# Another written-out order for the first part of an attention and Fourier-mixing kernel

## The chip, the cores and the metric

The kernel runs on one core of a Trainium2 chip. The metric is the time of one execution in device microseconds (us). The core has five engines that run side by side and wait for one another by semaphores: PE (matrix products), ACT (elementwise functions), DVE (elementwise and reductions), POOL (elementwise), and SP, which here only issues transfers (DMA). Products land in eight banks of an accumulation memory, and another engine has to carry them off before a bank is used again.

## The reference

An attention block with random features, then a bridge, a Fourier mix, a normalisation and a two-layer MLP, all in float32:

```python
q_s, k_s = q * scale, k * scale                  # (8, 8, 576, 64), omega (128, 64)
def phi(x):
    h = einsum('bhsd,md->bhsm', x, omega) - sum(x * x, -1, keepdims=True) / 2
    return exp(h - max(h, -1, keepdims=True)) / sqrt(128)
kv, z = einsum('bhsm,bhsd->bhmd', phi(k_s), v), sum(phi(k_s), 2)
out = einsum('bhsm,bhmd->bhsd', phi(q_s), kv) / (einsum('bhsm,bhm->bhs', phi(q_s), z) + 1e-6)

x = heads of out side by side                     # (8, 576, 512)
u = x + real(fft(fft(x, axis=1), axis=2))
un = (u - mean(u)) / sqrt(var(u) + 1e-6)          # over the last axis
result = u + maximum(un @ w_ch1, 0) @ w_ch2       # (512, 2048), (2048, 512)
```

The two weight matrices arrive as float64.

## The kernel before, in words

The kernel has two parts, one after the other, each with an order of its own.

**The first part** ends at about 418 us. For each of the 8 batches it takes the 8 heads in 4 pairs (`attn`). A pair's k and q are loaded by SP (L499, L502) into `kq` and turned on PE (L642); the turned tiles are evicted as `kqT` (L658 on ACT, L656 on DVE). L737 forms the products with omega, L679 (DVE) the maxima, L696 (ACT) the exponentials `e`; L772 sums `kv`, L820 and L828 form the output, and L845 (ACT) or L849 (DVE) divide it into `x`, a tile that holds all heads of a batch (`x0` and `x1` in turn). The chip's omega itself is loaded by L518 and turned once at L620 (`first`). `warm` (L611) is six products of a tile of zeros, whose results nobody reads; each shows as two passes in the trace.

When the four pairs of a batch are done, `mix` does its Fourier transform by table products. It folds rows that mirror each other (L876 to L905 on DVE or POOL), multiplies by cosine and sine tables along the model axis (L939, result `y`, evicted at L969) and along the sequence (L999 and L1010). `residual` combines the two products of each of three chunks: L1048 (ACT) copies one out of its bank, L1053 and L1056 (DVE) form sum and difference, L1065 and L1066 (DVE or POOL) add them to `x`. What is then in `x` goes to a buffer `us` in device memory by SP (L1080). A middle slice goes by L1035 into a buffer `uh`, and L1091 copies that, in mirrored order, from `uh` into `us`: it has to wait for both stores of L1035 to land.

Beside that the first part narrows the weights from float64 to float32 (`narrow`: L564 on POOL or L566 on ACT, then L569 to L578 on DVE, then L582), forms sums of blocks of the second weight matrix (`w2_parts`, L1550), and passes four blocks of 128 tokens through the MLP in the plain way (`plain_of`: L1233 turns, L1299 is the first layer, L1281 or L1283 the relu, L1324 the second layer, L1338 adds the residual, L1115 stores the result). The last of these blocks is what PE does last in the first part. For the next 4 times 512 tokens it also normalises twelve half-blocks ahead (`ahead`, L1662 to L1676): ACT sums (L1662, L1665), POOL works out the factor (L1667 to L1669), ACT scales (L1671), DVE turns (L1674), SP stores (L1676). These use free `kq`, `kqT` and `ur2` tiles.

**The order of the first part** is written out by hand, as text. The work is a set of generators (streams); each gives one step at a time, with the engines on which the step may run. `Listing.run` holds a list of streams, each with its next step, and `PICKS` says which to take next: one character for each step, whose position in an alphabet is 36 times the choice of engine plus the stream's place in the list. `BANKS` is the bank of each step that takes one. `FORMS` says, for PE steps that can be cut in several ways, which cut: W is whole, C cuts the output into two halves of 64 columns, R and Q are the two cuts of L737 (20 passes over 128 columns or 32 over 64 for a group of four), and lower case letters stand for the middle of a mix. `BETWEEN` places the pieces of `ahead` after so many steps taken. Every engine executes its instructions in that order, so an instruction that waits holds what is behind it on its engine:

```python
def picked(text, n):
    if n == 1:
        return [divmod(DIGITS.index(c), 36) for c in text]
...
    listing.run(
        [first(), loads(), loads_v(), load_tables(), frames(), plain_norms(), mixing()]
        + [pairs(i) for i in range(NS)]
        + [w2_parts(), weight_sums(), block_norms(0, mlpp), plain(), weights(), warm()],
        picked(PICKS, 1),
        BANKS,
        betweens(BETWEEN),
    )
    early.close()
```

**The second part** takes the remaining tokens through the MLP by products of block sums in which seven products stand for eight (L1794 and L1946 first layer, L2247 second layer). `early.close()` gives up the tiles of the first part's loads, attention, mix and plain MLP, and the second part's tiles (`hid`, `so5`, `so6`, `so3`, `rx`, `s`, `wl`) lie in the same memory. Its first instructions are L2367 (`wash`, which clears banks), L1794, L1826 and L1819 (ACT, evictions, the second into `s`), L1749 (DVE and POOL, sums of weight blocks into `rx` and `so`), L1837 (DVE), L1924 (ACT) and L1946. Its loads of second-layer weights are L2142. It has order texts of its own (`PICKS2`, `BANKS2`, `BETWEEN2`).

Of the kernel before, what the change touches and what calls it, by code (L numbers as in the profile page):

```python
# [41 lines left out]
class Clock(NamedTuple):  # L42
# [23 lines left out]


PICKS = (
    "40e0fff03eafdaege3OcdceefdcOdeccfgda37ghj0gjj7hlP79aj7ik97i8S7efhjffeHldffiehdjfdOihgihidaKedbhhciff"
    "ecgOfeejdfdPdeeedgifdffdefd8aiii88jhd8jP8b99i8e8jcddghjgheiifcOcdciieicgPgdefJcdghbkededfgcRbggb79ij"  # L70
    "8hi7hjafN9Haj9gfffeg8eif8hcej1jccc7ehidbhffLigebfbe6766gggfcbjahj9Ofghhjj8dQkkgT6jghff8de6dUjfhbgegh"
    "cefhafjUf8jgciSjOckkhjakkaeikggjlioklnhSgodoXON7l7l6nnj9icadc97cibf98ejH88a7edhMlhkmjjaQVijihkkfplSm"
    "okliljjilVaghVhnmljkmpjkhhnmkimlgglmbjpjjQ9d9alafhhdjlaMdjback0j766k7lh4g896ck6gkki77gij5ijhgj6dimni"
    "3ndjgi6Kc4jldlKikbkaijLhf75dcjlmklk36ci45jciekajkkkk5kihokeaeoLaioNlencidonbSiljjcmjjkboijTUUhgcfkik"
    "hiflkmeFF99nol5m8jT7naabda89Rbj97ecdl8cjilOgifkQb4acahg57ebbgabgdjkdTkk6eceebb5f9dg4R6ce486ggg6egfhh"
    "fg4g9egf5cbdhgPRhhcgjhggejigibLmHnbedijj6NOb7biihi9bgihMkaffPa8cijdhbdghbaeibNefffacjicigifi99975ih5"
    "jgj8699ajfg6g7fgefd65bO6Kalkkgd5jgjikagfldliPJpeoaeeefgdejadgilgScljiii5e65k56kl57k7j67S9lilk9gliih6"
    "ffkgec4fg4dbgg7fedaiP5gfbheefilddddddeghg9kbfncgghcfkkafkagGngb65p5Hopoj4bhoanbelli68bjjl5b7dlhighhi"
    "lflhpkgiWomjknmmmkimnjbjhn9jkmFKkfFgedccff6Wf7idUVhi8Th3fogbqp8fgmkeSdjna7ckenoghmnmffnjeo79q6547oa4"
    "nlkpd7aceonnc8blSVicilbhmjim8fh7SnnIl5mUkfjgfhhfhihg8ghfbS4kjf83j4lllb79jei8mnkblfnmmiolpilOUi9Mh5l5"  # L80
    "pmnaem79jjVmkbblek5iji9a9kffTgjikhiShfgjafhgfigh4g50PPP0ba5Pdh9dghdK77hgfdcbg8OO988jMehefibjjkellfcc"
    "PcdhQMihfQcffbKCf82b3c98cbcdcd6a299efgddbJaGQQbefLa9ecf74gg986HRgf9idg8kQeheff7be6ff2e5cc8fbcgdKP8f8"
    "9hN9Lc999bddcHcNb7Oc9effegd7ibhQeQ8haf7ccghhlUikhHW5lWmm5dkMQGM71fS6d1gdb99747ifddhIfdhhdhfdbihgiljn"
    "gWgijgg93ekKl8kEhIIbT3jjKgkb9k9eTfhkhlje34m49974iG66h68faHe6e7a79982975aI94a39c8cM8b4aa7ab984fge8eLM"
    "98b86ce8PbFPc9cbe6cKPf3a9b94fIdIQeJKbd876eJPdc5fNb7ffbf9JSS8RiLa4a7gPbajfgg8gdfhg2i2787Hf6OcdIN5d3LH"
    "accd46ddeKK72dJc7bbaa4bb9a9bc7c0777dghhdf7Bfddebd76ff1fddIe9949438686bc6aca85348dHcG7a5be957b55d1544"
    "9Gc1F5a9a68446344584584E59189970955888574443113301110"
)

BANKS = (  # L90
    "0102346120164024306243643016204164024320632462014021604606245062345042604670426420340267407231640260"
    "4524016460620240674206206415704602546064320143607264506402346234062732017426042106147026740260462462"
    "0410652604632452017205467402624060404256174302642060245016745202642016420634520520650162505605260250"
    "1675602501605204672016204567627450264102316742067460260462045642062637230724672402630145420640106240"
    "5264023026731602454230412046450416725730620424670121726154305610207453"
)

FORMS = (  # L100
# [6 lines left out]
)  # L107


# [2354 lines left out]
```

## Time and profile before

| | us |
|---|---|
| median of 3 runs | 1117.52 |
| lowest and highest run | 1115.76, 1120.93 |
| the profiled execution, its own time | 1114.35 |
| its span, from the first to the last instruction | 1112.6 |
| first part (end of the last L1324) | 418.5 |
| PE busy | 1093.4 |
| DVE busy | 885.9 |
| ACT busy | 539.1 |
| POOL busy | 390.4 |

The durations of the profile come from the one profiled execution. In its rows, times are microseconds from the start of the span unless they are marked as ns; a row of the timeline gives start, duration, engine, line and operation, output and inputs by their names in the program, the tile sizes, how many instructions run in a row are grouped (x12), and, in brackets, how long the engine stood idle before and what released it. PEld is the loading of stationary tiles into PE, beside the products; SPq and ACTq mark the issue of a transfer. The granted clock is the share of full speed at which PE was allowed to run; it is 1.00 throughout. T in the text is the end of the last L1324, where the first part's work on PE ends.

### The profile page before, as it was taken

What the parts mean: (1) busy time and instruction counts of PE and PEld (TensorE: products, weight loads), DVE (VectorE), ACT (ScalarE), POOL (GpSimd) and SP (SyncE); (2) the same over time, 40 slices, a digit from 0 to 9 for tenths busy, and PEclk for the clock granted to TensorE, in tenths of its full rate; (3) what the DMA queues carried; (4) which work ended last, traced back from release to release, by engine and by line L of the source; (5) the groups of instructions that cost most, each with busy time, mean ns of one, the idle gap of its engine ahead of it and who ended that gap; (6) DMA issues with size and microseconds to landing.
All of it is one profiled execution on the core that took longest, in us unless ns stands there. A gap on an engine that the chain in (4) does not pass through costs nothing.

```text
span 1112.6 us, 41751 instructions
## 1 busy us (share of the span) xinstructions
PE 1093.4 (98%) x17507; PEld 934.7 (84%) x17507; DVE 885.9 (80%) x1685; ACT 539.1 (48%) x1644; POOL 390.4 (35%) x404
## 2 busy tenths in 40 slices
PE   8999999999999999999999999999999999999998
PEld 6788888878869666799998888998667999667998
DVE  6999999996676766688697777898667898668895
ACT  6998898856635464624214453223563223341221
POOL 2343443644473346634513455000365000152000
PEclk9999999999999999999999999999999999999999
DMA  7856767575675668798898768757678757556553
GB/s 230 229 183 182 241 182 220 162 212 160 221 231 187 188 169 314 236 300 287 247 303 300 211 200 260 213 155 237 206 216 262 220 154 223 167 158 220 151 158 113
DMA packets 196588, 236.77 MB, mean 213 GB/s; under 512 B 53808, under 2 KB 120624, under 8 KB 196400
## 3 DMA queue, kind: packets, MB, share of 16 engines
q1 hardware_dynamic: 195904, 233.83, 68.7%
q8 instruction: 138, 2.26, 0.9%
q14 instruction: 50, 0.41, 0.1%
q10 hardware_dynamic: 496, 0.26, 0.1%
HBM read 182.13 MB, written 56.10 MB: 214 GB/s over the span
## 4 chain that ended last, share of the span: by engine, by line
PE 90%; ACT 4%; DVE 3%; DMA 2%; issue 1%; SPq 0%; POOL 0%; DVEq 0%; ACTq 0%
PE banks L2247 30%; PE banks L1794 27%; PE banks L642 5%; PE banks L737 5%; PE banks L1324 5%; PE banks L1299 4%; PE banks L1946 4%; PE banks L772 3%; PE banks L820 2%; ACT e L696 2%; PE banks L999 1%; PE banks L939 1%; DMA kq<-in_q_dram 1%; DVE nmx L679 1%; PE banks L953 1%
## 5 line engine op out<-in xcount | busy, mean ns | idle before, releaser
L2247 PE MATMUL banks<-wl,sums 128*64 128x128 f32 x3584 | 217.5, 273 | 0.1
L2247 PEld LDWEIGHTS banks<-wl,sums 128*64 128x64 f32 x3584 | 201.6, 137 | 2.1 <-issue 0.5
L696 ACT ACTIVATE e<-banks,nmx 128x128 f32<-128x128 f32 x576 | 164.3, 426 | 21.8 <-DVE nmx L679 20.8
L679 DVE TENSOR_REDUCE nmx<-banks 128x8 f32<-128x1024 f32 (+1 forms) x96 | 89.3, 951 | 18.5 <-PE banks L737 15.4
L2247 PE MATMUL banks<-wl,hid 128*64 128x128 f32 x1536 | 99.0, 273 | 0.5 <-DVE part L2222 0.5
L2247 PEld LDWEIGHTS banks<-wl,hid 128*64 128x64 f32 x1536 | 88.0, 137 | 1.8 <-DVE part L2222 0.7
L1794 PE MATMUL banks<-unw,wxw 128*64 128x256 f32 x704 | 86.2, 379 | 0.0
L2217 ACT ACTIVATE s<-banks 128x128 f32<-128x128 f32 x112 | 30.9, 277 | 109.8 <-PE banks L2247 109.8
L737 PE MATMUL banks<-om,kqT 64*64 64x128 f32 (+1 forms) x1804 | 80.1, 276 | 2.5 <-issue 1.1
L737 PEld LDWEIGHTS banks<-om,kqT 64*64 64x64 f32 (+1 forms) x1804 | 66.2, 148 | 13.0 <-issue 4.8
L2247 PE MATMUL banks<-wl,hx 128*64 128x128 f32 x1152 | 73.6, 273 | 0.4 <-DVE part L2222 0.4
L1794 PEld LDWEIGHTS banks<-unw,wxw 128*64 128x64 f32 x704 | 53.3, 137 | 22.0
L1794 PE MATMUL banks<-rx,wxw 128*64 128x256 f32 x576 | 71.7, 379 | 0.0
L1794 PE MATMUL banks<-ttw,wxw 128*64 128x256 f32 x576 | 70.6, 379 | 0.0
L1819 ACT ACTIVATE s<-banks 128x512 f32<-128x512 f32 x65 | 38.5, 596 | 64.9 <-PE banks L1794 59.8
L2247 PEld LDWEIGHTS banks<-wl,hx 128*64 128x64 f32 x1152 | 65.4, 137 | 1.2 <-DVE part L2222 0.6
L1299 PE MATMUL banks<-unT,w 128*64 128x128 f32 (+1 forms) x720 | 64.7, 276 | 1.8 <-DVE qeT L656 1.8
L582 POOL TENSOR_TENSOR w<-w,raw 128x512 f32<-128x512 f32 x28 | 37.7, 1357 | 77.4 <-DVE raw L576 74.5
L2296 POOL TENSOR_TENSOR more<-more,part 128x512 f32<-128x512 f32 x2 | 2.7, 1336 | 172.8 <-ACT part L2289 172.8
L1299 PEld LDWEIGHTS banks<-unT,w 128*64 128x64 f32 (+1 forms) x720 | 58.6, 160 | 5.3 <-issue 2.3
L1794 PEld LDWEIGHTS banks<-rx,wxw 128*64 128x64 f32 x576 | 44.0, 137 | 17.6
L1794 PEld LDWEIGHTS banks<-ttw,wxw 128*64 128x64 f32 x576 | 44.0, 137 | 17.6
(289 smaller groups left out, 2413.3 us busy)
## 6 DMA issues: line engine op xcount, KB each, us to landing
wl<-w2l SPq DMA_DIRECT2D x245, 256.0 KB, 3.9
wxw<-w1x SPq DMA_DIRECT2D x120, 256.0 KB, 3.2
raw<-in_moe_w_ch_dram SPq DMA_DIRECT2D x32, 512.0 KB, 5.3
kq<-in_k_dram SPq DMA_DIRECT2D x32, 288.0 KB, 4.4
kq<-in_q_dram SPq DMA_DIRECT2D x32, 288.0 KB, 4.7
vd<-in_v_dram SPq DMA_DIRECT2D x32, 288.0 KB, 5.5
ur<-us SPq DMA_DIRECT2D x30, 256.0 KB, 4.6
w2l<-sums SPq DMA_DIRECT2D x14, 512.0 KB, 4.9
```

Of the source, the lines that this page charges most:

```text
L582: eng.tensor_tensor(out=dst, in0=dst, in1=lof, op=ALU.add)
L642: nc.tensor.transpose(ps[:, (j - j0) * 128 : (j - j0 + 1) * 128], src(j), ident[:])
L679: nc.vector.tensor_reduce(nmx[:, :, 0:num], pps[:, :, 0 : MF * num].rearrange("p b (c m) -> p b c m", m=MF), axis=AX.X, op=ALU.max, negate ...
L696: nc.scalar.activation(out=e[:, c + (i if num == 1 else 0), :], in_=pps[:, i, MF * c : MF * c + MF], func=AF.Exp, bias=nmx[:, i, c : c + 1],)
L737: nc.tensor.matmul(pps[cols, c, MF * m : MF * m + MF], lhsT=kqT[rows, j, cols], rhs=om2[rows, :],)
L772: nc.tensor.matmul(kvp[cols, i, 0 : D + 1], lhsT=feature(r)[rows, cols], rhs=vds[n % NV][rows, r, :], start=(r == 0), stop=(r == R - 1),)
L1299: nc.tensor.matmul(hp[cols, 0:TP], lhsT=w1[:, dc, 128 * fc : 128 * fc + 128][:, cols], rhs=unTs[key][:, dc, :], start=(dc == 0), stop=(dc ...
L1324: nc.tensor.matmul(yp[cols, 0:DM], lhsT=hs[fc][:, 128 * i : 128 * i + 128][:, cols], rhs=w2[:, fc, :], start=(fc == 0), stop=(fc == NFC - ...
L1794: nc.tensor.matmul(ps[half, span * f : span * f + span].rearrange("f (b q) -> f b q", q=Q), lhsT=left[:, P * f : P * f + P][:, half], rhs= ...
L1819: nc.scalar.activation(out=s[:], in_=ps, func=AF.Copy)
L1946: nc.tensor.matmul(cell[half].rearrange("f t (b q) -> f t b q", q=Q), lhsT=w[:, d, col : col + 128][:, half], rhs=right[:, :, d].rearrange ...
L2247: nc.tensor.matmul(ps[half, 0:128], lhsT=left[:, f][:, half], rhs=wls[head(j), i, n][:, f], start=start and f == 0, stop=(f == 3), skip_gr ...
```

## The change

The change replaces the three texts `PICKS`, `BANKS` and `FORMS` of the first part. It changes no function, and `BETWEEN` and the texts of the second part stay. Cut to the first and last lines of each text, the diff is:

```diff
 PICKS = (
-    "40e0fff03eafdaege3OcdceefdcOdeccfgda37ghj0gjj7hlP79aj7ik97i8S7efhjffeHldffiehdjfdOihgihidaKedbhhciff"
...
-    "98b86ce8PbFPc9cbe6cKPf3a9b94fIdIQeJKbd876eJPdc5fNb7ffbf9JSS8RiLa4a7gPbajfgg8gdfhg2i2787Hf6OcdIN5d3LH"
-    "accd46ddeKK72dJc7bbaa4bb9a9bc7c0777dghhdf7Bfddebd76ff1fddIe9949438686bc6aca85348dHcG7a5be957b55d1544"
-    "9Gc1F5a9a68446344584584E59189970955888574443113301110"
+    "0ff0e5cedce04aadbcN9dcffaddhfS9ibbbKdd4Pg9hagdfgKb9ggahbd9gMadgccfbiiiaifjS9fdeic8gada1ebggb9gi7RJb7"
...
+    "a57cKC7McF57ab7aa6ccRee7edhLahagghffdcKg1Qbd9d2hehhfee21bKcPgQQ8PPP9Oeadde1259E47eDNeeOeeeeeOeOeObac"
+    "ceNadeed3cddNcdMM4123a8G646826J9abcdefg506GeddhQagPAf67cheij7jHdj79T3aMj86gb9egacQabI59ccc478a3b57c2"
+    "a895423345888557206477H8H737715355F652556562314232010"
 )
 BANKS = (
-    "0102346120164024306243643016204164024320632462014021604606245062345042604670426420340267407231640260"
...
+    "3041346021064104260174062306201464602367026426450642014202640141050640264236204206126042301672042064"
...
 )
 FORMS = (
-    "5W 2R W Q 2W 2Q 2W Q W Q 2W Q W C Q 3W 2R 3W 3Q W C 2W Q 3W C 2Q 2W Q W Q 3W 4Q C 2W Q 5W 3Q C W WR 3W WQ W R "
...
-    "2R 2Q 9W 5W czC 6C 2W WQ 5C CQ W C Ccz 3C W 3C Ccz 2C Ccz 9W 3W"
+    "5W 2R W R 2W 2Q 2W 2Q 4W Q C Q 3W 2R 3W 3Q C 4W Q 2W C 2Q 2W 2R 4W 4Q C 3W Q 4W 3R C W WR 3W WQ W Q 2Ccz Q W 2R "
...
+    "C 2Ccz 9W W 3C Ccz 9W 3Q 7W WQ 5C CQ 4Q Ccz 6W 2Q 3C Ccz 2C 2R 2Q C 9W 8W czC 9C 9C 4C 4W CQ 5W WQ C 2Ccz czC 3C"
 )
```

Since the orders are data, what the change does is read from the instructions of the two built programs, engine by engine:

- On PE, the transposition of omega (L620) stands ahead of the six products of `warm` instead of behind them and four transposes of k.
- L1299 runs in 128 whole and 256 half-width instructions instead of 152 and 208, L1324 in 42 whole and 44 half instead of 56 and 16, L737 in 224 wide and 704 narrow groups' passes instead of 250 and 652.
- Work that may run on several engines is shared out anew: L564 (POOL) 28 instead of 8 and L566 (ACT) 4 instead of 24; L876 on POOL 11 instead of 5 and on DVE 5 instead of 11; L845 (ACT) 80 instead of 40; L1283 (ACT) 32 instead of 44.
- Near the end of the first part fewer L1324 stand behind the last mix: 12 instead of 32. On ACT the last two pieces of `ahead` stand ahead of the L1048 of the mix's last two chunks, and on SP the last stores are, in order: two L1035, L1091, two L1676, L1115, and four L1080.

The line numbers of this text are those of the program before; in the changed one they are one lower from the texts on, because `PICKS` is a line shorter.

More of the change, by code (lines that the diff above doesn't have):

```diff
@@ L68 @@
 PICKS = (
-    "40e0fff03eafdaege3OcdceefdcOdeccfgda37ghj0gjj7hlP79aj7ik97i8S7efhjffeHldffiehdjfdOihgihidaKedbhhciff"
[L70 to L83, printed above, removed]
@@ L84 @@
-    "gWgijgg93ekKl8kEhIIbT3jjKgkb9k9eTfhkhlje34m49974iG66h68faHe6e7a79982975aI94a39c8cM8b4aa7ab984fge8eLM"
-    "98b86ce8PbFPc9cbe6cKPf3a9b94fIdIQeJKbd876eJPdc5fNb7ffbf9JSS8RiLa4a7gPbajfgg8gdfhg2i2787Hf6OcdIN5d3LH"
-    "accd46ddeKK72dJc7bbaa4bb9a9bc7c0777dghhdf7Bfddebd76ff1fddIe9949438686bc6aca85348dHcG7a5be957b55d1544"
-    "9Gc1F5a9a68446344584584E59189970955888574443113301110"
+    "0ff0e5cedce04aadbcN9dcffaddhfS9ibbbKdd4Pg9hagdfgKb9ggahbd9gMadgccfbiiiaifjS9fdeic8gada1ebggb9gi7RJb7"
+    "79h8fbj0k9fj9bh7Ih9iaacahbcfbc8ahiekalf6hgc6hghi89kJkhcfjjTbdiihgjgJceiRdidlkgdeeigim8UcldcddgjcddeR"
@@ new lines @@
+    "8hcebO99ahgig9h9ibigggf98h1hdaR9g6eidhiiiije8i6h7diSdjdjdeaHQi9bhg9dh7kg9mmcjab6afminUi9l9kfjgf8icJf"
+    "f7giibUfmXjcOhmedj69lggji6jkghj7ebmc9n6gekjelcmnnklkcbjaf7jmRIlkbgibidRcfifljHQelilmeVTjdeTaikhldklm"
+    "lhkVaelfgeljliafdfgfQfSkhHea7hhaldjemdkkkTh9lfNQdTggfjjj9abk89gjl505j6d8kddkc87j5djlc7cakba56kicajcd"
+    "mcmddnccJRmRd5Idf3SgIbk9K6fllmangmfnk6aQd8hkjleggmmleenkm6k8HnbfTlk8emallmWjdjkjlggmmfhnjm3SjgeRi9dj"
+    "ldkkchhffjchljLTgVkljfgclkJkTkj96ccm86l5Heod8ak3Hjakjkjkjk89ki9hbg6effffa5fcf4Qfgc6Kbgdhabci8cahLdgf"
@@ new lines @@
+    "de6O84fNf56fgiO96hh8k6Sffhg9i9bJkadhbdjighT6aSejii6a8hdcfj7egfdcdbOb8edf8cdecbgjcjhdbgmmicaGh7Qn4eGI"
+    "7L7khjNci7fbghhRih79cd7mhnaibkonoagU6ihdgJfGIQjaddi55ialcmWbgiimUegjlc8iVdWmWffbkdjdeei9ckaG7d68al99"
+    "kilO7gij4bMd7dcf7eci5idhcc4jdibedejlhfl6df6lebNjfkNjgdjd9kgUf5gehilklba9499fmdfllVhill8akmlbnib6nkih"
+    "lll8fHihk7ejjaclUkhdglikjhll84higl5felh6iWgNiNi3njYbgcdcPnbdicpqigqnWP9apedcknkpfilSaiekgnhbnXHdimim"
+    "fi4lJcmllkT6f8Ucllcf9cfhmVhbfomo9paeeRmjmdVfnng65gk45jieli3jUbfk5k7Ql7hmm77gOidjlilnjkV55oNghnfflmnj"
@@ new lines @@
+    "lmc7cOgfj55ikk8fkmmjeJbgQglcmmeSkghhkkjglhmbi9ecmeli9g4iijdcicciiihghffi5miQjae7Pkck9EfRafejkSggejQM"
+    "eeaOa8fLb7ee49d9dacdef8cf7agafgP5Qg8edf8K8efe9hdJObcdhRQdg9dbd9fgfdKcP9bgcdgcabP9PPaaP49aeLccddecc1c"
+    "879ef7bbeecbb3ebdfdM6L8ef0ef16LhK1gThe6k66k2M66dHdgiFM8bhhe4jdjflc6aglm99dfM6lWPbe2Sc5D84kajNaiijfQb"
+    "8a5kjhlgllJddge4mUlcfM8OMfSe9hc4ea9f7f8g82919a56P27cFa792ccI9d685897aebJcc5Ib8b8fgegd98a28efNd6dMfOa"
+    "a57cKC7McF57ab7aa6ccRee7edhLahagghffdcKg1Qbd9d2hehhfee21bKcPgQQ8PPP9Oeadde1259E47eDNeeOeeeeeOeOeObac"
@@ L94 @@
-    "1675602501605204672016204567627450264102316742067460260462045642062637230724672402630145420640106240"
-    "5264023026731602454230412046450416725730620424670121726154305610207453"
+    "3041346021064104260174062306201464602367026426450642014202640141050640264236204206126042301672042064"
+    "2014016260462042672042620451356250642314036702674260140642306034021673045624610421640726346204604202"
+    "6067167240632405134750643260204624604625736503642060264701450724604672726014012562040126073640620603"
@@ L96 @@
+    "7242060231206421065206450142065026406351074626410167406202456240642643725732013640746527464214506254"
+    "3046206457234065234236024623627045010760462257236410571734054134616406"
 )
 FORMS = (
[6 rows of a table removed]
[5 rows of a table added]
 )
```

2 lines of the change are left out of this document (removed), and 7 rows, old and new, of the table FORMS.

## The prediction

> **What bounds the kernel now.** I read the head of the page first, then a table of busy time by stretch, then the timeline at the two ends of the first part. The page's first two parts and the engine line of its chain:
>
> ```profile
> span 1112.6 us, 41751 instructions
> PE 1093.4 (98%) x17507; PEld 934.7 (84%) x17507; DVE 885.9 (80%) x1685; ACT 539.1 (48%) x1644; POOL 390.4 (35%) x404
> PE 90%; ACT 4%; DVE 3%; DMA 2%; issue 1%; SPq 0%; POOL 0%; DVEq 0%; ACTq 0%
> ```
>
> The next view is split at 100 and 420 us; the first part ends a little before 420. Its columns are stretch, length, then busy time of PE, PEld, DVE, ACT and POOL, the granted clock, DMA share and GB/s.
>
> ```profile
> 0.00:100.00 100.00, 90.96 (x2042) 76.47 (x2046) 85.47 (x172) 86.16 (x314) 35.66 (x44) 1.00 0.72 207
> 100.00:420.00 320.00, 315.19 (x5595) 259.82 (x5587) 260.16 (x595) 213.93 (x739) 150.91 (x166) 1.00 0.64 197
> ```
>
> The reader is to see that PE sets the time, that PE idles only 100 - 90.96 = 9.0 us in the first stretch and 320 - 315.19 = 4.8 us in the second, and that PE's instructions in the part that changes aren't shortened by a slow clock. A new order of the same steps has these to win: 13.8 us of PE idle, and whatever PE work the new forms save. It can lose at any place where PE is now covered. So I looked for places where it uncovers PE: the start, and the seam to the second part.
>
> **Forms and turns.** In the built programs the number of places in the first part where PE changes its tile shape goes from 206 to 182. What one change costs, and what a form costs:
>
> ```profile
> 74.49 0.60 PE L642 MATMUL banks<-ident,e 128*128 128x128 f32 x4
> 74.92 0.27 PE L642 MATMUL banks<-ident,kq 128*128 128x128 f32 x1
> 75.03 0.60 PE L642 MATMUL banks<-ident,e 128*128 128x128 f32 x4
> 75.56 0.85 PE L820 MATMUL banks<-kv,qeT 128*64 128x65 f32 x21
> 398.37 1.95 PE L1299 MATMUL banks<-unT,w 128*64 128x128 f32 x32
> 402.85 1.95 PE L1299 MATMUL banks<-unT,w 128*128 128x128 f32 x16
> ```
>
> Four transposes followed by the same shape start 74.92 - 74.49 = 0.43 us apart from what follows; four followed by a 64-column tile, 75.56 - 75.03 = 0.53. A turn costs 0.10 us; 24 fewer give **-2.4 us**. The same L1299 step takes 1.95 us as 16 whole or 32 half instructions, so I cost the form itself at nothing. Its ends are -1, since some turns lie beside a wait, and -3.4, as turns between other shapes may cost more.
>
> **The start.** The rows of the timeline from 0 to 8 us, and, for the tile `om`, the time from issue to landing:
>
> ```profile
> 0.72 0.47 ACTq L518 DMA_DIRECT2D om<-in_omega_dram  x1
> 1.04 2.93 PE L611 MATMUL banks<-ur 128*128 128x128 f32 x12 [1.04 <-DVE ur L520]
> 3.90 0.64 PE L642 MATMUL banks<-ident,kq 128*128 128x128 f32 x4
> 4.37 0.27 PE L620 MATMUL banks<-ident,om 128*128 128x128 f32 x1
> 5.13 0.77 PE L642 MATMUL banks<-ident,kq 128*128 128x128 f32 x5 [0.48 <-DMA kq<-in_q_dram]
> DMA to landing us min/median/max: 3.2/3.2/3.2
> ```
>
> Before, PE fills the wait for the first loads with the six products of L611 (12 passes), and these end as k lands. In the changed program L620, which needs omega, stands first on PE, and the twelve passes stand behind it. Omega lands at 0.72 + 3.2 = 3.9, L620 takes 0.27, the passes again up to 2.93 - 0.27 = 2.7, so the first transposes of k start near 6.9 instead of 3.90: 3.0 later. The 0.48 us wait for q goes, as q has landed by then: **+2.5 us**. If the passes ran at the pace of 0.11 us that the transposes above show ((0.60 - 0.27) / 3) they would take 1.3, and the loss would be 1.1; 3.0 is the other end. L611's pace, 0.24 at its start, argues for the high side.
>
> **Inside the first part.** The change moves elementwise work between engines. The counts are of the built programs: L564 on POOL 8 to 28, L566 on ACT 24 to 4 (the same narrowing step), L876 on POOL 5 to 11 and on DVE 11 to 5; the other moves nearly cancel on POOL. One instruction of each costs:
>
> ```profile
> L564 POOL TENSOR_SCALAR w<-raw 128x512 f32<-128x512 f32 x8 | 12.9, 1613 | 19.8 <-DMA raw<-in_moe_w_ch_dram 19.8
> L876 POOL TENSOR_TENSOR half<-x 128x1024 f32<-128x1024 f32 x5 | 11.8, 2360 | 8.7 <-DVE mid L915 5.1 <-DMA kq<-in_q_dram 2.0 <-DVE rden L837 0.7
> L566 ACT ACTIVATE w<-raw 128x512 f32<-128x512 f32 x24 | 18.4, 777 | 3.9 <-DMA raw<-in_moe_w_ch_dram 3.9
> L876 DVE TENSOR_TENSOR half<-x 128x1024 f32<-128x1024 f32 x11 | 14.7, 1340 | 0.2
> L574 DVE TENSOR_SCALAR sign<-w x32: 426/428/1430, 15.7 to 242.6; 128x512 uint32<-128x512 uint32 x32
> ```
>
> POOL gains 20 x 1.61 + 6 x 2.36 = 46 us, against its 187 (35.66 + 150.91) in 420; it stays under 60%, so its own time is free while nobody waits for it. ACT sheds 20 x 0.78 = 16 us (much of it taken back by evictions, which are written out by hand as well), DVE 6 x 1.34 = 8. ACT is at 86% and DVE at 85% in the first 100 us, where PE's idle is largest, so this should shorten PE's waits for them: I take **-5 us**, about a third of the 13.8. No row prices it: -12 (nearly all idle goes) and +5 are its ends. For the upper end: L574 took 428 ns in the median and 1430 at worst, so something holds DVE now and then, and with a quarter more of POOL's work that may grow, on every such line. The Trainium skill's "SBUF — State Buffer", under "SBUF: two separate sides", says that DVE with two operands from that memory (or in a fast mode) and GpSimd lock one pair of ports for a whole instruction, the loser blocked; taken for each of the 26 added POOL instructions, with one of their lengths each, that speaks against this change by 46 us of DVE time. This trace shows one-instruction delays on L574 of up to 1.0 us, and a median without any.
>
> **The seam.** The second part's text is unchanged, but its tiles lie in memory that the first part held. In both built programs these instructions wait for every transfer that reads a first-part tile: ACT's first L1819, DVE's and POOL's first L1749, SP's first L2142. How that looks before:
>
> ```profile
> 404.64 13.90 PE L1324 MATMUL banks<-w,ht 128*128 128x512 f32 x32
> 416.58 0.53 SPq L1676 DMA_DIRECT2D turned<-kqT  x1
> 418.57 0.69 DVE L1338 TENSOR_TENSOR ur<-ur,banks 128x512 f32<-128x512 f32 x1 [2.02 <-PE banks L1324]
> 419.25 0.69 DVE L1749 TENSOR_TENSOR rx<-w 128x512 f32<-128x512 f32 x1
> 420.92 0.60 ACT L1819 ACTIVATE s<-banks 128x512 f32<-128x512 f32 x1 [0.29 <-PE banks L1794]
> 422.92 1.04 PE L1794 MATMUL banks<-unT,w1s 128*64 128x128 f32 x16
> 424.43 0.69 DVE L1837 TENSOR_TENSOR hid<-banks,s 128x512 f32<-128x512 f32 x1 [1.48 <-PE banks L1794]
> 426.40 1.90 PE L1946 MATMUL banks<-unT,w 128*64 128x256 f32 x16
> ```
>
> Call T the end of the last L1324: 404.64 + 13.90 = 418.5. The last transfer of the first part is L1676 (issued 416.58, landed 2.4 us later by the row of its kind below): T + 0.5. So the gate is open when PE gets there, thanks to 13.9 us of L1324 behind the last mix. In the changed order only twelve L1324 (12 x 13.90 / 32 = 5.2 us) stand behind the mix's last product, and everything that the mix leaves to do comes after. Its prices:
>
> ```profile
> 412.04 0.61 ACT L1662 ACTIVATE kqT<-kqT 128x512 bf16<-128x512 f32 x1
> 415.84 0.71 DVE L1674 STREAM_TRANSPOSE kqT<-kqT 128x512 f32<-128x512 f32 x1 [1.16 <-ACT kqT L1671]
> 402.15 0.52 DVE L1053 SCALAR_TENSOR_TENSOR bmp<-banks,bmp 128x65 f32<-128x65 f32 x2
> 402.54 0.28 DVE L1056 TENSOR_TENSOR bmp<-banks,bmp 128x128 f32<-128x128 f32 x1
> 405.97 0.41 DVE L1065 TENSOR_TENSOR x<-x,bmp 64x257 f32<-64x257 f32 x1
> L1035 SPq DMA_DIRECT2D uh<-x x16: 597/610/1497, 79.1 to 411.5; - x16
> DMA to landing us min/median/max: 3.2/3.9/6.1
> L1080 SPq DMA_DIRECT2D us<-x x48: 325/586/1198, 70.6 to 410.1; - x48
> DMA to landing us min/median/max: 1.7/3.2/4.9
> DMA to landing us min/median/max: 2.4/2.6/5.7
> ```
>
> (The landing lines belong to L1035, L1080 and L1676 in turn.) On ACT two early norms, L1662 to L1671, stand ahead of the L1048 of the last two chunks, 3.8 us each (412.04 to 415.84, where its L1674 starts), the first from T - 6.5: L1048 comes at about T + 1.3. DVE then does L1053 and L1056 four times (4 x 0.8), two L1674 (1.4) and four adds L1065/L1066 (1.6): done near T + 7.5. SP stores `uh7` (L1035, two, 0.61 each), the second issued near T + 7.6 and landed by T + 11.5. Next on SP is L1091, which reads `uh7` back and so waits for that landing; queued behind it are two L1676, L1115 and last four stores L1080, some 4.5 us of issue by 0.53 and 0.586 each. The last is issued near T + 15 and lands 3.2 later: **the gate opens near T + 18**. PE reached the leaf that needs L1819 at 422.92, T + 4.4; it now comes at 18 + 0.6, 14.2 later. Behind the gate DVE has four L1749 and L1837, five times 0.69 at least, ahead of L1924 on ACT and the product that ran at 426.40, T + 7.9: that comes at T + 21.5 at the earliest, rather T + 23, 13.6 to 15.1 later. I take **+15 us**; 13 (stores landing in 1.7, the residuals a little earlier) and 18 (6.1 for L1035) are the ends. PE is busy to the end after that and gives nothing back.
>
> Such an idle stretch, 13 us, the trace before doesn't have. After its only cold start L611 ran at 0.24 us a pass against 0.11, for 2.9 us; if the same follows the gate, half of 2.9 is lost: **+1.5 us**, with 0 and 3 as ends. The Trainium skill's "TensorE: Matmul & The Clock Gate", Part 1, "What's actually happening", makes the idle itself the cause (an idle window of about 3.4 us halves the clock until as long a busy one); by it the term is an estimated 1.7, without it 0. The trace agrees as far as the row of L611 goes.
>
> **Sum.** -2.4 + 2.5 - 5 + 15 + 1.5 = +11.6. The profiled execution took 1114.35, which gives 1126.0; the median of the runs shown is 1117.52, 3.2 above the profiled one, and on that footing it is **1129 us**.
>
> **The rivals.** *Ports.* POOL's added 46 us delay DVE, and DVE delays PE: if a third of it reaches PE, +15 in place of -5, 1149 at worst; with a tenth, 1139. For it: the 1430 of L574, DVE at 85%. Against: the median of 428. Chance 0.10. *The first part pays for the gate.* If the new order removes most of the 13.8 us and the residuals run ahead of my reckoning, the terms are -2.4 + 2.5 - 12 + 13 = +1, 1119, not slower; it decides where PE leaves the first part some 12 us earlier, before 407. For it: ACT and DVE are relieved; against: POOL is not, and the start already costs 2.5. Chance 0.13, some 1112 to 1123. *The gate doesn't bind*, as the stores land before PE reaches T + 4.4, which needs the mix's residuals done 14 us sooner than reckoned, or SP not held at L1091. Then -2.4 + 2.5 - 5 = -5, 1112.6, and by the idle's ends 1105 to 1122. This mechanism ends on the other side, not slower, with 0.05; nothing in the built order speaks for it. That the texts change nothing isn't possible: the built orders differ from the first PE instruction on.
>
> **How the numbers follow.** The forecast has 0.72. A measurement can tell about 0.5% (5.6 us) from no change: faster is below 1111.9, slower above 1123.1. Slower takes the forecast, save 0.03 at its low end, the ports, and 0.03 of the third case: 0.69 + 0.10 + 0.03 = 0.82. Same: that 0.03, 0.08 of the third case and 0.02 of the fourth, 0.13. Faster: the remaining 0.02 and 0.03, 0.05. The range: the terms' ends give 1119 to 1141 for the likeliest case; with most of the third case, 1117 to 1141 leaves out under 2 in 10.
>
> **What would show it.** Right: in the timeline after, PE L642 starts near 6.9; behind the last L1324 stand two leaves L1794, then PE idle of 12 to 15 us; ACT L1819 and DVE L1749 start together just after the last L1080 of SP lands; the stretch to T is 1 to 9 us shorter or about equal. Wrong: L1749 right behind L1338 and no gap on PE, or T later than 424, with DVE's L574 and two-operand lines longer than before.

## The result, and the profile after

| | us |
|---|---|
| before, median of 6 runs | 1117.56 (1115.52 to 1120.93) |
| after, median of 6 runs | 1148.6 (1143.94 to 1151.15) |
| ratio | 1.0271, 95% interval 1.0243 to 1.0298 |
| profiled execution after, its span | 1144.90, 1143.1 |

The changed kernel is 31 us slower, where 11.6 were forecast. The profiled executions differ by as much, 30.55 us, so they can be taken apart (each is some 3.5 us quicker than its kernel's median). First the head of the page after:

```profile
span 1143.1 us, 42068 instructions
PE 1103.2 (97%) x17659; PEld 961.4 (84%) x17659; DVE 902.1 (79%) x1695; ACT 532.6 (47%) x1641; POOL 438.6 (38%) x433
PE 61%; DVE 2%; POOL 1%; issue 1%; DMA 1%; SPq 1%; ACT 1%; ACTq 0%; DVEq 0%; POOLq 0%
```

PE's share of the span hardly changes, but POOL has 48 us more, and the chain of work that ended last can no longer be followed back to the start: PE carries 61% of the span in it, 90% before.

**The start**, from the timeline after (line numbers are one lower from here on):

```profile
3.95 0.45 PE L619 MATMUL banks<-ident,om 128*128 128x128 f32 x1 [3.95 <-DMA om<-in_omega_dram]
4.19 2.77 PE L610 MATMUL banks<-ur 128*128 128x128 f32 x12
6.75 2.13 PE L641 MATMUL banks<-ident,kq 128*128 128x128 f32 x9
```

PE waits for omega to 3.95, the twelve passes stand behind it, and k's first transposes start at 6.75 instead of 3.90.

**The seam**, from the timeline after:

```profile
427.35 5.32 PE L1323 MATMUL banks<-w,ht 128*64 128x512 f32 x24
438.53 1.27 SPq L1034 DMA_DIRECT2D uh<-x  x2
442.52 0.58 SPq L1090 DMA_DIRECT2D us<-uh  x1
445.27 2.51 SPq L1079 DMA_DIRECT2D us<-x  x4
450.94 0.69 DVE L1748 TENSOR_TENSOR rx<-w 128x512 f32<-128x512 f32 x1 [11.85 <-DMA us<-x]
451.04 0.60 ACT L1818 ACTIVATE s<-banks 128x512 f32<-128x512 f32 x1 [11.35 <-DMA us<-x]
451.69 1.97 PE L1793 MATMUL banks<-unT,w1s 128*64 128x128 f32 x16 [7.92 <-ACT s L1818]
457.37 1.89 PE L1945 MATMUL banks<-unT,w 128*64 128x256 f32 x16
```

T is 427.35 + 5.32 = 432.7, 14.1 us later than before (the 24 records are twelve half-width instructions; their 5.32 us had been reckoned as 5.2). The gate, as the prediction calls it, is the moment at which the second part may use the first part's memory. DVE and ACT both stand still for 11 us and are released by the same transfer, the last L1079, 18.3 us after T. After T the program takes 1143.1 - 432.7 = 710.4 us, before it took 1112.6 - 418.5 = 694.1: **the seam costs 16.4 us, the first part 14.1**. The windows up to T and from T on, before and then after, show what PE does in them (stretch, length, busy PE, PEld, DVE, ACT, POOL, clock, DMA share, GB/s):

```profile
0.00:418.50 418.50, 404.65 (x7599) 335.02 (x7600) 344.24 (x763) 300.09 (x1051) 186.58 (x210) 1.00 0.66 200
418.50:1112.60 694.10, 688.79 (x9911) 599.70 (x9908) 541.62 (x922) 239.06 (x593) 203.84 (x194) 1.00 0.72 221
```

```profile
0.00:432.70 432.70, 409.12 (x7750) 335.92 (x7751) 352.94 (x755) 292.68 (x1046) 230.06 (x235) 1.00 0.62 189
432.70:1143.10 710.40, 694.03 (x9910) 625.49 (x9909) 549.12 (x940) 239.88 (x596) 208.57 (x200) 0.99 0.70 218
```

Up to T, PE idles 23.6 us instead of 13.9 and is busy for 4.5 us more. From T on it idles 16.4 instead of 5.3 and is busy for 5.2 more. How the clock answers shows in the windows of the seam, in the same columns:

```profile
432.70:440.70 8.00, 4.28 (x37) 3.49 (x36) 5.62 (x19) 1.65 (x4) 3.26 (x6) 0.68 0.51 139
440.70:451.70 11.00, 3.08 (x37) 2.43 (x36) 0.73 (x2) 0.66 (x2) 0.00 (x0) 0.66 0.65 198
451.70:455.00 3.30, 3.30 (x24) 2.70 (x26) 3.30 (x4) 0.92 (x2) 2.33 (x2) 0.50 0.81 251
455.00:470.00 15.00, 14.81 (x148) 10.03 (x146) 10.22 (x10) 8.54 (x17) 14.14 (x10) 0.96 0.92 333
```

**Inside the first part**, three stretches of after, then the last two of before (its first is in the prediction), in the same columns:

```profile
0.00:100.00 100.00, 90.73 (x1998) 77.99 (x2002) 86.43 (x171) 83.53 (x306) 47.10 (x50) 1.00 0.72 204
100.00:250.00 150.00, 144.78 (x2977) 124.86 (x2967) 142.25 (x317) 109.87 (x401) 91.47 (x84) 1.00 0.62 188
250.00:420.00 170.00, 160.92 (x2679) 126.35 (x2678) 118.46 (x254) 91.98 (x323) 89.08 (x96) 1.00 0.57 184
```

```profile
100.00:250.00 150.00, 149.27 (x2960) 128.84 (x2951) 141.52 (x320) 123.12 (x433) 72.60 (x71) 1.00 0.68 203
250.00:420.00 170.00, 165.91 (x2638) 130.98 (x2638) 118.64 (x276) 90.81 (x307) 78.31 (x96) 1.00 0.62 191
```

In the first 100 us PE is busy for as long as before, in spite of the late start. From 100 to 250 us PE now idles 5.2 us instead of 0.7, behind that 9.1 instead of 4.1. DVE is at 95% in the middle stretch in both kernels, although the changed one gave it less to do, and ACT went down by 13 us without any gain. Groups of instructions on DVE tell why it has not become lighter: after, then before (busy us, mean ns, idle before):

```profile
L568 DVE TENSOR_SCALAR sign<-raw 128x512 uint32<-128x512 uint32 x32 | 19.2, 600 | 1.6 <-DMA raw<-in_moe_w_ch_dram 1.3
L1227 DVE TENSOR_SCALAR u<-u,mv,rstd 128x512 f32<-128x512 f32 x8 | 8.2, 1028 | 0.1
L1549 DVE TENSOR_TENSOR big<-w,big 128x512 f32<-128x512 f32 x5 | 7.1, 1471 | 0.1
```

```profile
L569 DVE TENSOR_SCALAR sign<-raw 128x512 uint32<-128x512 uint32 x32 | 16.2, 507 | 0.2
L1228 DVE TENSOR_SCALAR u<-u,mv,rstd 128x512 f32<-128x512 f32 x8 | 5.3, 661 | 1.1 <-POOL rstd L1226 1.1
L1550 DVE TENSOR_TENSOR big<-w,big 128x512 f32<-128x512 f32 x2 | 1.4, 683 | 0.0
```

The same instructions take longer. I call **DVE's surplus** what all DVE instructions up to T take over the shortest of the same operation and shape in the profiles that are compared; over the two kernels and the six runs on POOL and DVE below (runs 3, 4 and 7 to 10) it is 33.7 us before and 53.7 after (with fewer profiles in the comparison, or lines kept apart, some numbers quoted below are a few us lower). Only its differences are used.

### The profile page after: what moved, and what is told of

Read it like the earlier page. It is cut to its first block, busy times and chain, and to the rows that moved or that the text cites. A ratio compares the mean times of both kernels' runs of the same rounds, so it can differ in the third digit from the quotient of the medians.

```text
span 1143.1 us, 42068 instructions
## 1 busy us (share of the span) xinstructions
PE 1103.2 (97%) x17659; PEld 961.4 (84%) x17659; DVE 902.1 (79%) x1695; ACT 532.6 (47%) x1641; POOL 438.6 (38%) x433
## 4 chain that ended last, share of the span: by engine, by line
PE 61%; DVE 2%; POOL 1%; issue 1%; DMA 1%; SPq 1%; ACT 1%; ACTq 0%; DVEq 0%; POOLq 0%
PE banks L2246 29%; PE banks L1793 26%; PE banks L1945 4%; PE banks L1323 1%; POOL sums L1549 1%; DVE big L1549 0%; SPq L1108 0%; DMA us<-x 0%; DMA uh<-x 0%; PE banks L1298 0%; DMA u<-us 0%; DVE sums L1748 0%; DVE hid L1748 0%; DVE sums L1549 0%; DVE so L1748 0%
## 5 line engine op out<-in xcount | busy, mean ns | idle before, releaser
L695 ACT ACTIVATE e<-banks,nmx 128x128 f32<-128x128 f32 x576 | 159.7, 422 | 38.9 <-DVE nmx L678 37.4
L678 DVE TENSOR_REDUCE nmx<-banks 128x8 f32<-128x1024 f32 (+1 forms) x96 | 88.9, 950 | 16.0 <-PE banks L736 15.3
L1793 PEld LDWEIGHTS banks<-unw,wxw 128*64 128x64 f32 x704 | 60.4, 137 | 15.0
L1323 PE MATMUL banks<-w,ht 128*64 128x512 f32 (+1 forms) x172 | 60.1, 598 | 0.0
L1793 PEld LDWEIGHTS banks<-rx,wxw 128*64 128x64 f32 x576 | 49.4, 137 | 12.3
L1793 PEld LDWEIGHTS banks<-ttw,wxw 128*64 128x64 f32 x576 | 49.4, 137 | 12.3
```

Source lines behind the costliest of these rows:

```text
L678: nc.vector.tensor_reduce(nmx[:, :, 0:num], pps[:, :, 0 : MF * num].rearrange("p b (c m) -> p b c m", m=MF), axis=AX.X, op=ALU.max, negate ...
L695: nc.scalar.activation(out=e[:, c + (i if num == 1 else 0), :], in_=pps[:, i, MF * c : MF * c + MF], func=AF.Exp, bias=nmx[:, i, c : c + 1],)
L1323: nc.tensor.matmul(yp[cols, 0:DM], lhsT=hs[fc][:, 128 * i : 128 * i + 128][:, cols], rhs=w2[:, fc, :], start=(fc == 0), stop=(fc == NFC - ...
L1793: nc.tensor.matmul(ps[half, span * f : span * f + span].rearrange("f (b q) -> f b q", q=Q), lhsT=left[:, P * f : P * f + P][:, half], rhs= ...
```

## The experiments

Unless a run says otherwise, "the changed kernel" is compared by its median, 1148.6, and the kernel before by the median of the same chip's runs, 1115.7 to 1117.2. The changed kernel's six runs spread over 7 us, so a difference of four runs' from them is uncertain by 3 to 5 us. The orders are data, so the edits are given as what they do to the engines' lists, with the line numbers of the program before.

**1. The seam's stores.** In stores_first:

```diff
 SP, last of the first part:
-L1080 x2, L1035 x2, L1091, L1676 x2, L1115, L1080 x4
+L1080 x6, L1035 x2, L1676 x2, L1115, L1091
```

> The changed kernel, with SP's last four stores L1080 and the stores L1676 issued ahead of L1091 (the read-back of uh7), nothing else. In the changed kernel the second part's gate opened 18.1 us after T (T: end of the last L1324), as the last L1080 stood behind L1091, which waited for uh7 to land. If that wait is what holds the gate, the gate opens some 6 us earlier (the 3.4 us wait, L1091's issue of 0.6, and what the second store of uh7 then bounds), near T + 12: total 4 to 8 us less than the changed kernel. Rival: the gate is held by DVE's and ACT's residual work, and the transfers only happen to land last; then the gain is under 2 us.

1141.53 us (1137.26 to 1142.39), 7.1 less. In its profile T is at 432.2 and 703.3 us follow, where 710.4 did. The wait for `uh7` did hold the gate, as queued ahead of the stores.

**2. The start.** In omega_later:

```diff
 PE, first of all:
-L620, L611 x12, L642 ...
+L611 x12, L620, L642 ...
```

> The changed kernel with L620 (omega's transpose) behind the six products of L611 again, as before the change. L642 starts at 6.75 us in the changed kernel and at 3.90 before. If the start is simply added, L642 starts near 4.3 and the total falls by 2.5 us. Rival: the first loads and evictions set the pace of the first 30 us anyway, so the lead is lost by 50 us: total within 1 us.

1146.1 us (1144.31 to 1147.45), 2.5 less, as forecast; but the changed kernel's own runs (1143.94 to 1151.15) take it in, so this decides nothing. The splices (runs 11 to 14) test the start better.

**3 and 4. Who narrows.** The changed kernel with the narrowing given back, and the kernel before with it taken over:

```diff
 narrow_on_act, the changed order:        before_narrow_pool, the old order:
-L564 POOL x28, L566 ACT x4               -L564 POOL x8, L566 ACT x24
+L564 POOL x8,  L566 ACT x24              +L564 POOL x28, L566 ACT x4
```

> The changed kernel with 20 of the 28 narrowing steps L564 on POOL given back to ACT (L566), the same 8 left on POOL as before the change; place in the order, banks and forms stay. Theory of the ports: POOL's work holds DVE up. In the first part DVE's instructions took 48.0 us more than the shortest of their kind, 27.9 before the change. Giving back 32 us of POOL takes a good part of that away (to some 38) and the total falls by 5 to 10 us, although ACT gets 16 us more. Theory of the order: what costs is which waiting instruction stands ahead of which on an engine, not who does the narrowing; then DVE's surplus may fall, but the total stays within 3 us, or rises by ACT's load.

> The kernel before, with the same 20 narrowing steps moved from ACT (L566) to POOL (L564), nothing else. Theory of the ports: DVE's surplus in the first part rises from 27.9 us to some 38, and the total by 5 to 12 us. Theory of the order: the old order has room for it (POOL is busy 45% of the first part), total within 3 us, or below, as ACT sheds 16 us.

narrow_on_act took 1154.01 us, 5.4 more than the changed kernel, although DVE's surplus fell from 53.7 to 45.7. before_narrow_pool took 1121.3, ratio 1.0042 (1.0030 to 1.0055), 4.8 more than before, with the surplus up from 33.7 to 43.0 and 16 us less narrowing on ACT (20 x 0.78). So POOL's added work does lengthen DVE's, by 8 to 9 us for 32; but in the changed order the same work is worse on ACT, a rise that the theory of the order had allowed for. The theory of the ports was right on DVE's time in both orders, and on the total only nearly, in the old one.

**5. Places of the early norms.** In norms_later, the early norms' steps on ACT and what hangs on them move by up to 21 places in `BETWEEN`, for instance:

```diff
 ACT, near 401 us:
-L1662 L1665 (kq), L1283 x3
+L1283 x3, L1662 L1665 (kq)
```

> The changed kernel with only the places of the early norms' steps (the text BETWEEN) moved by a few steps in the last 60 us of the first part: each L1661/L1664 and L1670 on ACT now stands behind the evictions (L1236, L1282) that PE waits for, instead of ahead of them. In the changed kernel PE waited there 1.5, 1.4, 1.1 and 1.0 us for ACT's L1236 and L1282 (at 391, 403, 408 and 412 us) while ACT stood at an early norm that waited for POOL (6.2 us) or for its load (3.7 us). Theory of the order: T comes 3 to 6 us earlier, and the total falls as much. Theory of the ports: ACT only waits because POOL and DVE are late, T moves by under 1.5 us.

1148.3 us, no change (0.3). From 380 us to T, PE waited 5.0 us for ACT in the changed kernel and 4.8 for ACT and DVE here: the waits only went elsewhere, and this theory of the late waits fell.

**6. The whole seam.** tail_moved:

```diff
 as stores_first, and
-ACT: L1048 (c=0), two early norms, L1048 (c=2), L1048 (c=1)
+ACT: L1048 (c=0), L1048 (c=2), L1048 (c=1), two early norms
-PE:  two steps of L1324 ahead of the last mix's second L939
+PE:  these two behind its last L1010
```

> The changed kernel with three moves at its seam: SP's last stores ahead of L1091 (as in the run stores_first, which gained 7 us), the L1048 of the last mix's last two chunks ahead of the last two early norms on ACT, and two of the L1324 steps moved behind the last mix on PE (20 records behind it instead of 12). If the seam's 16.4 us (time after T, 710.5 against 694.0) is made by these three, the gate opens some 5 to 8 us earlier still than in stores_first: 695 to 699 after T, total 11 to 15 us less than the changed kernel. Rival: the last two norms, now later, hold the gate themselves by their stores L1676; then after T it stays at 702 to 705.

1133.62 us, 15.0 less. The timeline of this run:

```profile
427.96 9.00 PE L1323 MATMUL banks<-w,ht 128*128 128x512 f32 x32
440.88 0.60 SPq L1090 DMA_DIRECT2D us<-uh  x1
442.40 5.86 SPq L2141 DMA_DIRECT2D wl<-w2l  x7
443.08 1.09 PE L1793 MATMUL banks<-unT,w1s 128*64 128x128 f32 x16 [1.46 <-ACT s L1818]
```

The gate opens at 442.4, 5.4 us after T (437.0), PE waits 1.46 us for it instead of 7.92, and is not slow afterwards (1.09 for the product that took 1.97). After T it takes 1132.9 - 437.0 = 695.9 us, 14.5 less than the changed kernel and within 2 of the kernel before. (T itself differs from run to run: it is at 437.4 in norms_later's profile too, and at 432.2 in that of stores_first. So the seam's share is read from T on.)

**7 and 8. Less for POOL, nobody more.** In narrow_left_out and pool_relief, which leave out a part of the narrowing, so that only their time means anything:

```diff
-        if step.eng == POOL:                                       # 20 of 28 steps
-            nc.gpsimd.tensor_scalar(dst, hif, 2.0**-112, None, op0=ALU.mult)
+        pass
...
-        eng.tensor_tensor(out=dst, in0=dst, in1=lof, op=ALU.add)   # pool_relief alone: the 27 on POOL
```

> The changed kernel, with the first instruction (L564 on POOL) of 20 of the 32 narrowing steps left out and nothing in its place; L571 of these reads the raw word instead. So POOL has 32 us less and no other engine has more. Theory of the ports: DVE's surplus in the first part (its instructions' time over the shortest of their kind, 53 us in the changed kernel and 33 before it) falls to some 43, and T, 432.7, comes 5 to 9 us earlier, most of it in the first 250 us, where DVE is busy 95%. Theory of the order: T stays within 2 us.

> As narrow_left_out, and the 27 adds L582 of the narrowing on POOL left out too: POOL has 32 + 37 = 69 us less than in the changed kernel, no other engine has more. narrow_left_out took 6.3 us off DVE's surplus and 4.8 us off the total. Theory of the ports: twice the relief, DVE's surplus near 40 us and the total 8 to 13 us below the changed kernel. Rival: the narrowing's own chain (DVE and weights waiting for POOL) made that gain, then the second half gives 2 us or less more.

1143.82 us (4.8 less) and 1140.94 (7.7 less); the surplus fell from 53.7 to 47.3 and to 41.6. The middle window of pool_relief:

```profile
100.00:250.00 150.00, 147.77 (x2947) 126.10 (x2948) 140.29 (x326) 112.46 (x410) 49.49 (x55) 1.00 0.58 180
```

PE's idle time there is 2.2 us, of 5.2 in the changed kernel and 0.7 before. The first 32 us of POOL seem worth 4.8, the next 37 another 2.9, but either step alone is within the noise; the two together, 7.7, are clear of it and just under what the theory of the ports asked for (8 to 13). The rival, that the narrowing's own chain became shorter, asked for 2 or less from the second step, and 2.9 does not rule it out: both runs leave out steps of that chain.

**9 and 10. Less for DVE, in both orders.** after_sign_left_out and before_sign_left_out:

```diff
-        nc.vector.tensor_scalar(sign[:], bits, 0xFF800000, None, op0=ALU.bitwise_and)
```

> The changed kernel with one DVE instruction of each of the 32 narrowing steps left out (L574, 0.51 us, 16 us of DVE in the first 250 us), nothing in its place. If DVE's time is what PE waits for in the changed order, the total falls by 7 to 12 us. Rival, that other waits (ACT's place in the order) set the pace there: it falls by under 3 us.

> The kernel before with the same 32 instructions L574 left out, as the control: 16 us less of DVE. If the old order hides DVE behind PE, the total falls by under 4 us; if DVE sets the pace in the old order as well, by 7 to 12 us, as in the changed one.

The changed kernel gained 6.8 us (1141.79, just short of the 7 asked for), the kernel before 1.2 (1115.67, ratio 0.9992, 0.9980 to 1.0004). The same 16 us of DVE are all but covered in the old order, and some four tenths of them are on the path in the new one. tail_omega, the moves of runs 6 and 2 together, came with these:

> The changed kernel with the moves of tail_moved and of omega_later together; nothing is left out. If the seam and the start are independent prices, their gains add: 15.0 + 2.5 below the changed kernel, 1131 us. What stays above the kernel before, some 14 us, is then the inside of the first part. Rival: the start's gain is lost in the first 50 us, 1133.6.

1132.18 us (1131.96 to 1133.45), between the two forecasts and 1.4 below tail_moved, which is within the noise: with both moves 15.3 us are left above the kernel before.

**11 to 14. Splices.** The two orders hold nearly the same set of steps at every point (of the first 500, all but 5), so one can follow the other:

```diff
 steps           1-500   501-1300  1301-1853
 before          old     old       old
 changed kernel  new     new       new
+h_start         new     old       old
+h_start_omega   new, L620 behind L611    old   old
+h_mid           old     new       old
+h_end           old     old       new
```

> A splice: the first 500 of the 1853 steps in the changed kernel's order (to about 99 us), all others in the order of the kernel before, with its places of the early norms; engines, banks and forms come with each step (3 banks differ, as those written were taken). At 98.6 us both kernels were at the same step, though the changed one starts 2.9 us later, so this stretch should cost 0, and up to 2.5 us if the start's loss only shows later. Rival, that the lost lead of this stretch is what the rest suffers from: 8 us or more.

> A splice: steps up to 500 in the order of the kernel before, from there to step 1300 (about 100 to 265 us) in that of the changed kernel, the rest as before (9 banks differ). By the two profiles PE's idle time over its products was 11 us more in the changed kernel from 100 to 300 us. If the price is made by this stretch itself (DVE's surplus and the waits on ACT in it), the total is 7 to 11 us above the kernel before. Rival, that it comes with the changed first 100 us: under 3 us.

> A splice: the first 1300 steps in the order of the kernel before (to about 262 us), the rest and the places of the early norms as in the changed kernel (1 bank differs). The seam costs 15 to 16 us there; PE's waits from 300 us to T were 6 us more than before. If stretches only add up: 19 to 24 us above the kernel before. With h_start and h_mid the three should then make 31. Rival, that the late waits are carried over from the stretch before: 15 to 17.

> As h_start, with L620 behind L611 again (omega_later). In the changed kernel the first 100 us lose nothing although they start 2.9 us later, so the stretch itself is 2 to 3 us quicker than that of the kernel before: this splice should be 1 to 3 us below the kernel before. Rival: the first 100 us are set by the loads, and it is within 0.5 us of h_start.

h_start: 1116.48 us, ratio 1.0003 (0.9988 to 1.0017). h_mid: 1127.79, ratio 1.0097 (1.0073 to 1.0122), 11.0 more than before. h_end: 1137.17, ratio 1.0190 (1.0163 to 1.0217), 20.4 more. The three differences of medians (-0.3, 11.0, 20.4) make 31, and 31.0 was measured: within their uncertainty of some 5 us, the stretches add. h_start_omega, the one that might beat both, took 1115.69, ratio 0.9994 (0.9981 to 1.0006): not told apart from the kernel before, nor from h_start (0.8 us). One reserve: h_mid idles behind its second joint too, 5.2 us in this window of its profile, where the changed kernel idles 1.3 (48.73 busy of 50) and the one before 0.7 (49.26), so that 11.0 is rather a top value for the middle:

```profile
250.00:300.00 50.00, 44.79 (x881) 38.50 (x881) 37.56 (x70) 26.90 (x98) 24.24 (x24) 0.93 0.63 186
```

> As h_end (the first 1300 steps in the old order, the rest in the changed one; 20.4 us above the kernel before), with the three moves of tail_moved, which took 15.0 us off the changed kernel. If the seam is one price of its own, 20.4 - 15.0 = 5.4 remain above the kernel before, 1120 to 1124 us, for PE's waits between 262 us and T. Rival, that the order up to 1300 and the end's waits belong together: the moves take under 10 us off here, and it stays above 1127.

h_end_tail (the first 1300 steps old, the rest new with the moves of run 6): 1125.22 us, ratio 1.0079 (1.0049 to 1.0109), 9.6 more than before. The moves gave back 12.0 here, less than 15.0 and more than the rival's 10. Its profile tells where the 9.6 are:

```profile
415.02 9.00 PE L1323 MATMUL banks<-w,ht 128*128 128x512 f32 x32
431.80 1.97 PE L1793 MATMUL banks<-unT,w1s 128*64 128x128 f32 x16 [3.12 <-ACT s L1818]
```

T is at 424.0, 5.5 us later than before, and 1123.2 - 424.0 = 699.2 us follow, 5.1 more than before: PE still waits 3.12 us for the gate and its next product is slow. So only about half of what is left stands ahead of T, some 4 to 5.5 us; the other half is seam that the moves did not mend in this order.

**15 and 16. Order and shares apart.** In steps 501 to 1300, 72 steps have another engine in the changed kernel:

```diff
 steps 501-1300     order   engines
 before             old     old
 h_mid              new     new
+mid_order_alone    new     old
+mid_engines_alone  old     new
```

> As h_mid (steps 500 to 1300 in the changed kernel's order, the rest as before; 11.0 us above the kernel before), but each of these 800 steps on the engine that the kernel before gave it; 72 of them have another in the changed kernel, among them 14 narrowing steps that go from POOL back to ACT. If the engines' shares (POOL's work and what it does to DVE) make the price of this stretch: under 4 us above the kernel before. If the order itself makes it: 8 us or more, or above h_mid, as the order was made for the lighter ACT.

> The kernel before, every step in its old place, but the same 800 steps on the engines that the changed kernel gives them. If the shares make the price: 6 to 11 us above the kernel before, more than the 4.8 of the 20 narrowing steps alone. If the order does: 1 to 4 us, for the 14 narrowing steps among them (14/20 of 4.8 is 3.4).

1142.01 and 1142.86 us: 25.2 and 26.0 more than before, ratios 1.0223 (1.0184 to 1.0261) and 1.0221 (1.0193 to 1.0250). For mid_order_alone the theory of the order had asked for 8 us or more, which holds; the other three numbers were wrong, and neither theory foresaw 26.0 from the engines alone. The window of mid_engines_alone, then of mid_order_alone:

```profile
100.00:250.00 150.00, 131.86 (x2607) 114.42 (x2606) 129.78 (x274) 103.17 (x373) 83.79 (x76) 0.96 0.58 173
```

```profile
100.00:250.00 150.00, 137.50 (x2789) 117.68 (x2788) 127.30 (x279) 114.66 (x410) 63.92 (x60) 0.99 0.58 178
```

PE idles 18 and 12 us there, while DVE is less busy than in either whole kernel: the engines wait for one another in turn. The granted clock falls in these waits as well; 0.96 over 150 us is an estimated 6 us of PE's work lost. Here each share-out is good only with the order that it was made with, and so is each order.

## Why the prediction was right or wrong

**The seam: right, in place, size and mechanism.** Said: gate at T + 18, the product that needs `s` (the leaf) at T + 18.6, +15 and +1.5 for the clock. Measured: 18.3, 451.69 - 432.7 = 19.0, and 16.4 in all. PE's idle time came in three pieces (1.75, 1.97 and 7.92 us), near 11 us and not 12 to 15. The clock was 0.50 for the 3.3 us behind the gate and 0.96 for the next 15, an estimated 1.65 + 0.6 = 2.2 us of work lost. The Trainium skill's "TensorE: Matmul & The Clock Gate", Part 1, gives an idle window of about 3.4 us as the cause; the trace agrees in the main, with 0.50 behind the wait of 7.92 us and no slow product where the wait was 1.46 us, but the clock was at 0.68 already in the 8 us behind T, where no single wait was over 1.97 us. That the gate hangs on SP's order is shown by run 1 (7.1 us), and on the order on ACT and PE as well by run 6 (15.0 with all three moves; those of ACT and PE were not tried apart).

**The start: its size right, its worth wrong.** 2.85 us later were measured, 3.0 said. But the term +2.5 does not show in the sum: h_start, which starts late as well, is level with the kernel before, and the windows show as much busy time in the first 100 us as before. Where the lost lead goes is not shown: if the rest of that stretch were quicker, h_start_omega should gain it, and its 0.8 us are within the noise.

**The turns: not measured by themselves.** No run separates the -2.4. But PE's busy time up to T, which turns and forms were to shorten by that much, went up by 4.5 us, from 404.65 to 409.12. Each is one execution, and a second profile of the old order's steps (before_sign_left_out) has 406.77, so about half of the 4.5 may be chance; nothing of the saving shows.

**The inside: the step that failed.** I took -5 us, "about a third of the 13.8" of idle time, with ends -12 and +5. PE's idle time up to T went from 13.9 to 23.6 us instead, +9.7, of which the first 100 us have almost nothing. The fault is in the step that ACT is at 86% and DVE at 85%, both are given less, "so this should shorten PE's waits for them". DVE did not become lighter (its surplus rose by 20 us), and the step took the old order's slack for granted. The old order covers DVE so well that 16 us less of it bring 1.2; in the new one PE idles more in nearly every stretch, and the same 16 us bring 6.8. So the upper end +5 could not be right either: it priced POOL's effect on DVE, and not that DVE's time had come onto the path. The sign that the prediction named for being wrong came true: T later than 424, with DVE's lines longer. And its range was too narrow for its own terms: their ends, added up, reach from 1116 to 1146, not from 1119 to 1141.

**The rival of the ports: part of it.** That POOL's work lengthens DVE's is shown: 32 us more on POOL made DVE 9.3 us slower in the old order, 69 us less made it 12.1 us faster in the new; the time moved by 4.8 us in the one and 7.7 in the other. That the time moved through DVE, and not through the narrowing's own chain, is argued only. The Trainium skill's "SBUF — State Buffer", "SBUF: two separate sides", has the loser blocked for a whole instruction; these DVE rows have typical instructions at their old length and a few much longer, which agrees, but the total is 20 us of surplus for 44 us more of POOL, not an instruction's length for each. The rival's 1149 at worst was the time measured, but by luck: its part is 5 to 8 of the 31, and the seam and the order made the rest.

**The sum by what was measured.** Start 0, middle at most 11.0, end ahead of T some 4 to 5.5, seam 15 to 16.4. The ports' 5 to 8 lie within the first part's. **What stays open** is why PE waits more in the middle and at the end ahead of T: runs 15 and 16 show that in the middle it belongs to order and shares together, and run 5 that the early norms' places are not it. No run found a single wait that carries it.

## What to carry to other kernels

Before an order is judged by what each engine has to do, look for the instruction behind which memory is given up, and list everything that must land before it: work moved late on a side engine can open that gate later although PE's own list is shorter. And test how much slack an order has before pricing relief or load on a side engine: leave a known amount out in both versions (here 16 us of DVE were worth 1.2 and 6.8). A written-out order and its shares of the engines are one object; in the middle stretch here half of a new one (25 and 26 us) was worse than all of it (11).

## What the runs showed of the hardware that was not expected

One DVE row shows POOL's hold on DVE far more strongly than those that I had looked at. From the line's own view, after and then before (min/median/max in ns):

```profile
L1227 DVE TENSOR_SCALAR u<-u,mv,rstd x8: 508/762/2595, 103.9 to 416.4; 128x512 f32<-128x512 f32 x8
```

```profile
L1228 DVE TENSOR_SCALAR u<-u,mv,rstd x8: 539/542/1491, 102.0 to 401.7; 128x512 f32<-128x512 f32 x8
```

L574, on which I had rested, has a median of 428 ns before and 427 after and shows this only in its longest; the surplus has to be summed over all lines. The longest of these rows, with what POOL did at the time (from the timeline after):

```profile
403.48 2.73 POOL L875 TENSOR_TENSOR half<-x 128x1024 f32<-128x1024 f32 x1 [1.15 <-ACT ht L1282]
403.90 2.60 DVE L1227 TENSOR_SCALAR u<-u,mv,rstd 128x512 f32<-128x512 f32 x1
```

POOL's instruction ends at 406.21, and DVE's 0.29 us behind it. So it goes in the two traces as a whole. Up to T, 15 DVE instructions before and 43 after took 0.3 us or more over the shortest of their line and shape, 10.6 and 29.9 us in sum, which is nearly all of the 20 us by which the surplus rose. Every one of them started while a POOL instruction was running, as about half of all DVE instructions do (335 of 763 before, 391 of 755 after). 13 of the 15 and 32 of the 43 ended as if they had begun when a POOL instruction ended (to within 0.25 us); the others ran beside the narrowing step on POOL (L564, L563 after) and were slower without being held to its end.
